# Hand-written order for the last five units of a chunked mLSTM, and a regrouped merge and dispatch behind them

## The chip, the cores and the metric

One core of a Trainium2 chip (trn2) runs the whole program in one launch. The metric is the device time of an execution in microseconds, taken as the median of several runs. TensorE (PE) does the products, VectorE (DVE), ScalarE (ACT) and GpSimd (POOL) the rest; SyncE (SP) issues the DMAs.

## The reference

Three layers in a row, all in float32, on 3072 tokens (4 batches of 768) of width 320.

1. mLSTM: 32 heads (8 per batch) of width 40. Per step `m' = max(f + m, i)`, `C = exp(f + m - m') C + exp(i - m') v k^T`, `n` the same with `k` alone, `y = sigmoid(o) * (C q) / max(|n q|, 1)`.
2. Soft mixture of experts: `logits = x @ phi` (32 slots); a softmax over the tokens (down the columns) mixes tokens into slots (dispatch), eight experts with a hidden width of 1024 and a relu work on four slots each, and a softmax over the slots (along the rows) mixes the results back into tokens (combine).
3. MLP: `relu(x @ w_in)^2 @ w_out` with 2048 hidden columns.

The column softmax needs the maximum over all tokens, so the dispatch can't end before the last token of layer 1 is there.

## The kernel before, in words

Heads are taken in groups of three (the last, group 10, has two), time in six chunks of 128. A pair (g, c) of group and chunk is a unit; there are 66, the last six being (10, 0) to (10, 5). Each goes through the same steps. `e_u` makes the outer products of a chunk on PE, `e_uc` the running state from them (with a mask that keeps each head's own block), `e_mb` and `e_exp` the decay factors (PE, then ACT), `e_sel` their causal cut (POOL), `e_st` the scores (PE), `e_pm` their product with the factors (DVE), `e_inter` the part that comes from earlier chunks' state and `e_av` the part from the chunk itself (PE, both into one PSUM bank for a pair of chunks), `e_num` their sum. `fin(g)` then divides a group's sums by the denominators and multiplies them into the sigmoid in tile `x`.

The loop over the units (from line 947) issues the steps of different units interleaved, scores two units ahead and factors three. All other work of this time is held as generators ("fillers") that yield a letter for the engine they want next: the sigmoids, `fin`, layer 2's tokens of batches 0 to 2, `merge` (which brings the three batches' column maxima together, line 802) and `merge_tr` (transposes of batch 3, line 853). `filler` and `advance` take from them at fixed places of each unit. All waits on semaphores are set by the framework from the order of the program; every engine and SP's queue work in that order.

PSUM is divided into banks by tags: two of `mb`, `st` and `o` each, one `m`, and `ltb` for the logits. A `bank(tag)` that is asked for again waits for all readers of the old contents.

Behind the loop come the last unit's sum (`n1`), `fin_last(2)` for the last two chunks, and what is left of the fillers. Then the tail in straight code: `fold` (line 842) adds the three batches' dispatched rows into partitions 96 to 127; the last 80 columns of batch 3 are transposed (L1110) and copied (L1112); the last logits; the maximum (L1125), the exponentials (L1126), the product L1131 that brings the maxima of four row blocks together, transposes of the exponentials (L1138) and their copy `en` (L1139); the dispatch product L1153, copied by ACT (L1160) and DVE (L1161) from one bank; four products with `comb` (L1166, L1170) and the denominators' (L1171), copied into `sT01` and `sT2` (L1173, L1178); and `ffn_up(0)`, the experts' first product (L1204). `cbuild(tg)` prepares the combine weights of 512 tokens in three parts: a split on DVE (L1071, L1072), four transposes on PE (L1078), a copy on ACT (L1083). `warm(n)` issues n bfloat16 products on the identity (L200) that nobody reads. `ld_w1`, `ld_w2` and `load_wo` issue weight transfers on SP.

The division of the last chunks before, in a few lines:

```python
nc.vector.scalar_tensor_tensor(out=rc, in0=dn, scalar=-1.0, in1=dn, op0=ALU.mult, op1=ALU.max)   # L673
nc.vector.tensor_tensor(out=xv, in0=xv, in1=nv, op=ALU.mult)                                      # L675
nc.vector.tensor_scalar(out=rc, in0=rc, scalar1=1.0, scalar2=2.0, op0=ALU.max, op1=ALU.mult)      # L676
nc.vector.reciprocal(rc, rc)                                                                      # L678
nc.vector.tensor_tensor(out=xv, in0=xv, in1=rc.unsqueeze(3).to_broadcast(...), op=ALU.mult)       # L679
```

Of the kernel before, what the change touches and what calls it, by code (L numbers as in the profile page):

```python
# [44 lines left out]
def kernel(  # L45
# [465 lines left out]
    def e_uc(g, c):  # L511
# [4 lines left out]
        cb = cb01[g, c % 2] if g < 2 else wk.tile([120, nh, DV], F32, tag="cbd", name="cbd", bufs=2)  # L516
        if c == 0:
            nc.vector.tensor_tensor(out=cb[0:nd], in0=uv, in1=hv, op=ALU.mult)
        else:
            if units.index((g, c)) >= NU - 3:  # L520
                nc.vector.tensor_tensor(out=uv, in0=uv, in1=hv, op=ALU.mult)
                nc.vector.scalar_tensor_tensor(
                    out=cb[0:nd],
                    in0=cbds[g, c - 1][0:nd],
                    scalar=dec120[0:nd, g, c : c + 1],
                    in1=uv,
                    op0=ALU.mult,
                    op1=ALU.add,
                )
                cbds[g, c] = cb  # L530
                return
# [50 lines left out]
    def e_num(g, c):  # L582
# [10 lines left out]
        tmp = wk.tile([128, 2, nh, DV], F32, tag="tmp", name="tmp", bufs=1)  # L593
        if n == 1:
            nc.scalar.copy(nums[g][:, 0], pv[:, 0, 0])
        if g == NG - 1 and c == 3:
            for k in range(n):
                for j in range(nh):
                    q0 = 64 + h0 + j
                    nc.scalar.activation(  # L600
                        tmp[:, k, j], pv[:, 1, k, j], AF.Copy, scale=qt3[:, c - 1 + k, q0 : q0 + 1]
# [11 lines left out]
    def fin(g, c0=0, c1=NC):  # L613
# [23 lines left out]
        order = "GG" if g == NG - 1 else "GGDGDD" if len(css) == 3 else "GD" * len(css)  # L637
        k = {"G": 0, "D": 0}
        for e in order:
            yield e  # L640
            i, cs = k[e], css[k[e] if g < NG - 1 else 0]
            k[e] += 1
            if g == NG - 1 and i:
                xv = xb[B1][:, cs, DM - nh * D : DM].rearrange("p c (n d) -> p c n d", d=D)
                eng.tensor_tensor(out=xv, in0=xv, in1=numr[0], op=ALU.mult)
# [19 lines left out]
    def fin_last(k, mid):  # L665
# [4 lines left out]
        rc = wk.tile([128, 2, nh], F32, tag="rcl", name="rcl", bufs=1)  # L670
        nv = num[:, :, :, 0:D]
        xv = xb[B1][:, 2 * k : 2 * k + 2, hh * D : (hh + nh) * D].rearrange("p c (n d) -> p c n d", d=D)
        nc.vector.scalar_tensor_tensor(out=rc, in0=dn, scalar=-1.0, in1=dn, op0=ALU.mult, op1=ALU.max)  # L673
        next(mid)
        nc.vector.tensor_tensor(out=xv, in0=xv, in1=nv, op=ALU.mult)  # L675
        nc.vector.tensor_scalar(out=rc, in0=rc, scalar1=1.0, scalar2=2.0, op0=ALU.max, op1=ALU.mult)  # L676
        finish(mid)
        nc.vector.reciprocal(rc, rc)  # L678
        nc.vector.tensor_tensor(out=xv, in0=xv, in1=rc.unsqueeze(3).to_broadcast([128, 2, nh, D]), op=ALU.mult)  # L679

    def sigm(b):
        for c in range(0, NC, 2):
# [4 lines left out]
            if b == B1:  # L687
                xl = xb[b][:, c : c + 2, DM - groups[NG - 1][1] * D : DM]
# [24 lines left out]
    def logits(kts):  # L713
        for kt in kts:
            kn = KT[kt][1]
            for r in range(NQ):
# [84 lines left out]

    def merge():
# [20 lines left out]
        yield "N"  # L823
        tt3 = mp.tile([96, B1], F32, tag="tt3", name="tt3")
        nc.vector.tensor_tensor(out=tt3, in0=es3, in1=se3, op=ALU.mult)
        cb3 = mp.tile([96, B1, 32], F32, tag="cb3", name="cb3")
        nc.vector.tensor_tensor(
            out=cb3,
            in0=selF[0:96].unsqueeze(1).to_broadcast([96, B1, 32]),
            in1=es3.unsqueeze(2).to_broadcast([96, B1, 32]),  # L830
            op=ALU.mult,
        )
        yield "P"
        t = ltb
        nc.tensor.matmul(t[:, DM : DM + B1], lhsT=sel4f[0:96], rhs=tt3, start=True, stop=True)
        folds.append(cb3)
        yield "N"
        nc.vector.tensor_reduce(out=se4[96:128], in_=t[96:128, DM : DM + B1], axis=AX.X, op=ALU.add)

    folds = []  # L840

    def fold():
        t = bank("st")
        for b in range(B1):
# [3 lines left out]
            if b < B1 - 1:  # L848
                yield
        nc.scalar.copy(xs4[96:128], t[96:128, 0:DM])  # L850
        yield

    def merge_tr():
# [4 lines left out]
        yield "Q"  # L858
        logits([1])
# [83 lines left out]
    for i, (g, c) in enumerate(units):  # L943
# [16 lines left out]
        if i == NU - 2:  # L960
            done.add("last")
            advance("Q", 1)
# [64 lines left out]
        if g == NG - 1 and c in (2, 4):  # L1027
            finish(nm or ())
            nm = None
            f1 = fin(g, c - 2, c)  # L1030
            if c == 2:
                add(f1, ("fin", g), [("sig", B1)])
            else:
                for _ in range(3):
                    next(f1)
# [8 lines left out]
    n1 = e_num(*units[NU - 1])  # L1044
    next(n1)
    finish(n1)
    fin_last(2, f1)
    while fillers:
        advance("W")
        filler("QPNADngG")  # L1050
# [17 lines left out]
    def cbuild(tg, get):  # L1068
        ct = call[:, 4 * tg : 4 * tg + 4, :].unsqueeze(2).to_broadcast([128, 4, 2, 32])
        chl = cp_.tile([128, 4, 2, 2, 32], F32R, tag="chl", name="chl", bufs=2)  # L1070
        nc.vector.tensor_copy(chl[:, :, :, 0, :], ct)  # L1071
        nc.vector.tensor_tensor(  # L1072
# [14 lines left out]
        cbuild(1, lambda: bank("o")),  # L1087
# [5 lines left out]

    def cgo(*tgs):
        for tg in tgs:
            next(cbs[tg], None)
# [3 lines left out]
    for n in (4, 5):  # L1100
        ld_w2(w2p[n], *w2o[2 + n])
    dumt = bank("mb")
    warm(4, dumt)
# [26 lines left out]
    tm = bank("m")  # L1130
    nc.tensor.matmul(tm[:, 0:4], lhsT=sel4f, rhs=mxr, start=True, stop=True)  # L1131
    rm = ca.tile([128, 1], F32, name="rm")
    nc.vector.tensor_reduce(out=rm, in_=tm[:, 0:4], axis=AX.X, op=ALU.max, negate=True)
# [7 lines left out]
    tr_el(0)  # L1141
    es = ca.tile([128, 1], F32, name="es")
    nc.scalar.activation(es, mx4, AF.Exp, bias=rm)
    nc.scalar.copy(el[:, 1, :], lt)
# [4 lines left out]
    next(fd)  # L1149
    xx = bank("st")  # L1150
    for u in range(2):
        for r in range(NQ):
            nc.tensor.matmul(  # L1153
                xx[32 * r : 32 * r + 32, 0:DM],
                lhsT=en[:, 0, u, 32 * r : 32 * r + 32],
# [424 lines left out]
```

## Time and profile before

| | |
|---|---|
| median of 3 runs | 385.25 us (385.08 to 386.76) |
| the profiled execution's own time | 386.99 us |
| its span in the profile | 385.3 us |
| busy share of the span | PE 97%, PEld 87%, DVE 69%, ACT 66%, POOL 27% |
| instructions | 9126 |

A row of a timeline tells when a group of like instructions on one engine began, how long it took with its tail, its line, what it writes and reads, its shape and count; in brackets how long the engine had been idle before it and whose work ended that. Neighbouring groups on PE overlap, since the next begins before the tail of the last is out. The lengths of PE's instructions are modelled.

### The profile page before, as it was taken

To read this page: it belongs to the slowest core of one execution; us is meant where nothing else is said; L and a number is where in the kernel's file an instruction comes from. 1 tells how busy PE (TensorE), PEld (TensorE's weight loads), DVE (VectorE), ACT (ScalarE), POOL (GpSimd) and SP (SyncE) were. 2 spreads that over 40 slices of the span, in tenths; PEclk is the share of its full clock that TensorE was granted. 3 is DMA by queue.
4 is the path that set the end of the run, shared out by engine and by line. 5 is a ranking of instruction groups with operands and counts; after the bars stand their busy time and mean duration, and the time that the engine had idled before them with its cause. 6 is when DMAs were issued, how large, how long until landed. Compare 5 with 4: busy or idle time off the path is not lost.

```text
span 385.3 us, 9126 instructions
## 1 busy us (share of the span) xinstructions
PE 374.1 (97%) x3419; PEld 333.8 (87%) x3419; DVE 265.9 (69%) x597; ACT 256.1 (66%) x585; POOL 102.5 (27%) x208
## 2 busy tenths in 40 slices
PE   8899999999999999999999999999999999999996
PEld 6789999889888886445699899999999999999996
DVE  7878888879888577758688965555555555555551
ACT  7689766668656854455697976676676667667662
POOL 4656866865686466000000000000000000000000
PEclk9899999999999999999999999999999999999999
DMA  6777898899959998599000010020010001002001
GB/s 187 246 267 230 276 308 244 240 331 336 313 173 364 330 350 307 191 382 373 1 2 0 2 68 3 0 70 1 2 53 17 1 2 68 2 1 70 1 2 68
DMA packets 19541, 56.62 MB, mean 147 GB/s; under 512 B 2481, under 2 KB 7561, under 8 KB 19113
## 3 DMA queue, kind: packets, MB, share of 16 engines
q1 hardware_dynamic: 19497, 56.04, 42.8%
q8 instruction: 27, 0.44, 0.5%
q14 instruction: 17, 0.14, 0.1%
HBM read 52.10 MB, written 3.93 MB: 145 GB/s over the span
## 4 chain that ended last, share of the span: by engine, by line
PE 78%; DVE 9%; ACT 4%; POOL 4%; issue 3%; DMA 2%; SPq 0%; DVEq 0%; POOLq 0%; ACTq 0%
PE ps_mb L1478 18%; PE ps_st L1478 17%; PE ps_lt L1478 9%; PE ps_st L474 6%; PE ps_o L1404 4%; PE ps_o L574 3%; PE ps_o L559 3%; PE ps_st L1282 2%; PE ps_m L1404 2%; DVE x L656 2%; DVE p L486 2%; PE ps_st L502 2%; ACT w L457 2%; PE ps_lt L717 1%; POOL w L464 1%
## 5 line engine op out<-in xcount | busy, mean ns | idle before, releaser
L1428 DVE CAST hi<-ring 128x512 fp32r<-128x512 f32 x93 | 39.7, 427 | 60.9 <-ACT ring L1427 52.7
L1429 DVE TENSOR_TENSOR los<-ring,hi 128x512 fp32r<-128x512 f32 x96 | 66.5, 692 | 9.8
L457 ACT ACTIVATE w<-ps_mb,qt 128x128 f32<-128x128 f32 x192 | 56.6, 368 | 15.8 <-PE ps_mb L443 10.4
L1409 ACT ACTIVATE ring<-ps_o 128x512 f32<-128x512 f32 x64 | 38.3, 599 | 34.1 <-PE ps_o L1404 34.1
L1427 ACT ACTIVATE ring<-ring 128x512 f32<-128x512 f32 x93 | 58.8, 632 | 3.0
L474 PE MATMUL ps_st<-par 120*128 120x128 f32 (+1 forms) x384 | 57.6, 286 | 0.0
L1478 PE MATMUL ps_mb<-wohlh,hi 128*128 128x320 f32 x160 | 49.4, 310 | 0.0
L1478 PE MATMUL ps_mb<-wohll,hi 128*128 128x320 f32 x160 | 49.3, 309 | 0.0
L1478 PE MATMUL ps_mb<-wohlh,los 128*128 128x320 f32 x160 | 49.2, 309 | 0.0
L474 PEld LDWEIGHTS ps_st<-par 120*128 120x128 f32 (+1 forms) x384 | 48.6, 194 | 0.0
L1478 PE MATMUL ps_st<-wohll,hi 128*128 128x320 f32 x144 | 44.7, 310 | 0.0
L1478 PE MATMUL ps_st<-wohlh,hi 128*128 128x320 f32 x144 | 44.5, 309 | 0.0
L1478 PE MATMUL ps_st<-wohlh,los 128*128 128x320 f32 x144 | 44.5, 309 | 0.0
L464 POOL TENSOR_SCALAR_AFFINE_SELECT w<-w 128x384 f32<-128x384 f32 (+1 forms) x66 | 36.4, 552 | 19.4 <-ACT w L457 13.6
L486 DVE TENSOR_TENSOR p<-ps_st,w 128x384 f32<-128x384 f32 (+1 forms) x66 | 35.4, 537 | 3.7 <-POOL w L464 2.7
L1409 ACT ACTIVATE ring<-ps_m 128x512 f32<-128x512 f32 x32 | 19.2, 599 | 18.2 <-PE ps_m L1404 18.2
L1478 PEld LDWEIGHTS ps_mb<-wohll,hi 128*128 128x128 f32 x160 | 29.9, 187 | 1.5
L1478 PEld LDWEIGHTS ps_mb<-wohlh,hi 128*128 128x128 f32 x160 | 30.0, 188 | 0.0
L1478 PEld LDWEIGHTS ps_mb<-wohlh,los 128*128 128x128 f32 x160 | 30.0, 188 | 0.0
L574 PE MATMUL ps_o<-par,p 128*64 128x41 f32 x768 | 29.0, 232 | 0.0
L1478 PEld LDWEIGHTS ps_st<-wohll,hi 128*128 128x128 f32 x144 | 27.0, 187 | 2.1 <-issue 0.6
L574 PEld LDWEIGHTS ps_o<-par,p 128*64 128x64 f32 x768 | 25.1, 137 | 3.9
(287 smaller groups left out, 776.1 us busy)
## 6 DMA issues: line engine op xcount, KB each, us to landing
ring<-in_w_dram SPq DMA_DIRECT2D x22, 640.0 KB
stage<-in_w_in_dram SPq DMA_DIRECT2D x10, 512.0 KB
par<-in_w_dram SPq DMA_DIRECT2D x6, 640.0 KB
out_dram<-ring SPq DMA_DIRECT2D x24, 160.0 KB
par<-in_v_s_dram SPq DMA_DIRECT2D x9, 369.0 KB
par<-in_k_s_dram SPq DMA_DIRECT2D x9, 360.0 KB
x<-in_o_gate_dram SPq DMA_DIRECT2D x9, 320.0 KB
par<-in_k_t_dram SPq DMA_DIRECT2D x23, 120.0 KB
```

The source lines that it names most:

```text
L457: nc.scalar.activation(w[:, j, :], mb[:, 128 * j : 128 * j + 128], AF.Exp, bias=qt3[:, c, h0 + j : h0 + j + 1])
L464: nc.gpsimd.affine_select(out=w, in_=w, pattern=[[0, nh], [1, 128]], compare_op=ALU.is_ge, fill=0.0, base=0, channel_multiplier=-1)
L474: nc.tensor.matmul(st[:, 128 * j : 128 * j + 128], lhsT=kbd[g % 2][0:nd, j, ts_], rhs=qin[g][0:nd, ts_], start=True, stop=True,)
L486: nc.vector.tensor_tensor(out=p, in0=sts.pop((g, c))[:, 0 : nh * 128].rearrange("p (n t) -> p n t", n=nh), in1=ws.pop((g, c)), op=ALU.mult,)
L559: nc.tensor.matmul(pos[g, c // 2][:, o0 : o0 + nv], lhsT=qin[g][0:nd, 128 * c : 128 * c + 128], rhs=cbds[g, c - 1][0:nd], start=True, stop ...
L574: nc.tensor.matmul(po[t0 : t0 + 64, o0 : o0 + DV], lhsT=p[:, j, t0 : t0 + 64], rhs=vin[g][:, c, j, :], start=True, stop=True,)
L1404: nc.tensor.matmul(t, lhsT=gst[n][:, 128 * k : 128 * k + 128], rhs=cst[tg], start=True, stop=True)
L1409: nc.scalar.activation(r, t, AF.Relu)
L1427: nc.scalar.activation(r, r, AF.Square)
L1428: nc.vector.tensor_copy(hi, r)
L1429: eng.tensor_tensor(out=lo, in0=r, in1=hi.bitcast(F32), op=ALU.subtract)
L1478: nc.tensor.matmul(acc[u][:, 0:DM], lhsT=l_[:, 128 * u : 128 * u + 128], rhs=wohl[r_, f // 8][:, f % 8, :], start=(f == 0 and a == 0), sto ...
```

## The change

- `e_uc` makes the state with two DVE instructions (mask on the products in PSUM, then the decayed sum) for the last five units, before for the last three. The others use one on DVE and a mask on POOL.
- The loop stops ahead of the last five units, and their steps are written out in an order by hand. `step` takes a filler's next parts.
- `e_num` of group 10 scales the state's part on ACT for chunks 1 and 3 (before for 3 alone).
- `fin(9)` adds its last third on POOL (with the sigmoid's +1 done beforehand on ACT); `fin(10)` is gone: `fin_last` divides all three pairs of chunks, of the first two both multiplies on POOL.
- The merge stops at the exponentials; `rest` makes the fold's weights and the denominators' terms behind `fin_last`, and their product is `tm[:, 16:19]`, in the bank of the maxima's product. The three folds come together.
- The logits' second third comes behind the last transposes; of the last third two row blocks go ahead of the third.
- The transposes of the exponentials stand ahead of the maxima's product; the dispatch product is done in two column halves in two banks, the products with `comb` in two banks.
- The eight `warm` products of the tail are gone, and one block of combine transposes moves behind `ffn_up(0)`, whose terms come in the order 0, 2, 1, 3, 4. Two w2 transfers move ahead of two `load_wo`.

```diff
-            if units.index((g, c)) >= NU - 3:
+            if units.index((g, c)) >= NU - 5:
...
-        if g == NG - 1 and c == 3:
+        if g == NG - 1 and c < NC - 1:
...
     def fin(g, c0=0, c1=NC):
-        order = "GG" if g == NG - 1 else "GGDGDD" if len(css) == 3 else "GD" * len(css)
+        order = "GGDGDX" if g == NG - 2 else "GGDGDD" if len(css) == 3 else "GD" * len(css)
...
-    def fin_last(k, mid):
+    def fin_last(k):
...
+        if k < 2:
+            nc.scalar.activation(rc, dn, AF.Abs)
+        else:
+            nc.vector.scalar_tensor_tensor(out=rc, in0=dn, scalar=-1.0, in1=dn, op0=ALU.mult, op1=ALU.max)
+            nc.vector.tensor_tensor(out=xv, in0=xv, in1=nv, op=ALU.mult)
+        (nc.vector if k == 2 else nc.gpsimd).tensor_scalar(
+            out=rc, in0=rc, scalar1=1.0, scalar2=2.0, op0=ALU.max, op1=ALU.mult
+        )
+        if k < 2:
+            nc.gpsimd.tensor_tensor(out=xv, in0=xv, in1=nv, op=ALU.mult)
+        yield
         nc.vector.reciprocal(rc, rc)
+        (nc.vector if k == 2 else nc.gpsimd).tensor_tensor(out=xv, in0=xv, in1=rb, op=ALU.mult)
...
-    for i, (g, c) in enumerate(units):
+    for i, (g, c) in enumerate(units[: NU - 5]):
...
+    e_u(g, 1)
+    e_mb(g, 4)
+    e_st(g, 3)
+    while w1q:
+        ld_w1(*w1q.pop(0))
+    ld_w2(w2p[2], *w2o[4])
+    e_uc(g, 1)
+    e_pm(g, 3)
+    e_exp(g, 4)
+    step("merge")
+    e_av(g, 0)
+    e_av(g, 1)
+    step("tr", 2)
+    e_inter(g, 1)
+    e_sel(g, 4)
+    step(f9, 3)
+    e_u(g, 2)
+    e_mb(g, 5)
+    e_st(g, 4)
+    e_uc(g, 2)
+    e_pm(g, 4)
+    e_exp(g, 5)
+    e_inter(g, 2)
+    e_sel(g, 5)
+    n1 = e_num(g, 1)
     next(n1)
+    step(f9, 2)
+    e_u(g, 3)
+    e_st(g, 5)
+    e_u(g, 4)
+    ld_w2(w2p[3], *w2o[5])
+    e_uc(g, 3)
+    e_pm(g, 5)
     finish(n1)
+    e_av(g, 2)
+    e_av(g, 3)
+    e_inter(g, 3)
+    e_uc(g, 4)
+    fl = [fin_last(k) for k in range(3)]
+    step(f9, 2)
+    next(fl[0])
+    n3 = e_num(g, 3)
+    next(n3)
+    e_inter(g, 4)
+    e_av(g, 4)
+    e_av(g, 5)
+    e_inter(g, 5)
+    finish(fl[0])
+    finish(n3)
+    next(fl[1])
+    step("tr", 5)
+    n5 = e_num(g, 5)
+    next(n5)
+    finish(fl[1])
+    finish(n5)
+    finish(fl[2])
...
-    for n in (4, 5):
+    for n in range(4, 8):
         ld_w2(w2p[n], *w2o[2 + n])
-    dumt = bank("mb")
-    warm(4, dumt)
+    rest = rests.pop()
+    next(rest)
...
-    next(fd)
-    cgo(0)
-    logits([2])
+    logits([1])
+    logits([2], (0, 1))
+    tt3 = next(rest)
+    logits([2], (2,))
     load_wo(xTw[:, 0 : SLOT // 2], 6, 2)
     next(fd)
-    warm(3, dumt)
+    next(fd)
+    tm = bank("m")
+    nc.tensor.matmul(tm[:, 16 : 16 + B1], lhsT=sel4f[0:96], rhs=tt3, start=True, stop=True)
...
     tr_el(0)
+    nc.vector.tensor_reduce(out=se4[96:128], in_=tm[96:128, 16 : 16 + B1], axis=AX.X, op=ALU.add)
+    nc.tensor.matmul(tm[:, 0:4], lhsT=sel4f, rhs=mxr, start=True, stop=True)
+    nc.vector.tensor_reduce(out=rm, in_=tm[:, 0:4], axis=AX.X, op=ALU.max, negate=True)
     nc.scalar.activation(es, mx4, AF.Exp, bias=rm)
+    finish(fd)
...
+    cgo(0)
+    for m, cs in enumerate((slice(0, 128), slice(128, DM))):
+        xx = bank("st")
...
+        (nc.vector.tensor_copy if m else nc.scalar.copy)(xs4[0:96, cs], xx[0:96, cs])
+    nc.tensor.matmul(tm[:, 8:9], lhsT=sel4f, rhs=tt, start=True, stop=True)
+    tk = [bank("mb"), bank("o")]
...
+        nc.vector.tensor_copy(sk[kt], tk[kt][:, 0:32].rearrange("p (e i) -> p e i", i=4))
...
+    cgo(0, 1)
     load_wo(x3.rearrange("p c d -> p (c d)")[:, 0 : SLOT // 2], 4, 2)
-    for n in (6, 7):
-        ld_w2(w2p[n], *w2o[2 + n])
-    cgo(1, 0)
...
-    def ffn_up(fh, ms_=range(5)):
+    def ffn_up(fh, ms_=(0, 2, 1, 3, 4)):
...
-    cgo(1, 2)
+    cgo(0, 2)
...
+    cgo(1, 1)
```

## Rows read from the trace of the kernel before

**Rows 1.** Busy time by stage: stage, length, engines, granted clock, DMA share, GB/s.

```profile
142.90:150.00 7.10, 6.84 (x94) 5.81 (x93) 6.21 (x25) 3.60 (x14) 4.36 (x12) 1.00 0.80 273
155.00:160.10 5.10, 4.60 (x42) 2.90 (x41) 2.46 (x13) 2.38 (x7) 0.00 (x0) 1.00 0.33 89
160.10:182.20 22.10, 22.10 (x240) 9.67 (x239) 16.70 (x43) 11.93 (x21) 1.90 (x2) 1.00 0.94 374
190.00:380.00 190.00, 189.31 (x1231) 184.54 (x1230) 115.85 (x203) 129.62 (x223) 0.00 (x0) 1.00 0.05 18
```

**Rows 2.** Chain that ended last, 145 to 161 us: start, length, what.

```profile
145.31 0.51 PE ps_st L474 x4
...
145.93 0.30 DVE cu L533
```

**Rows 3.** Timeline of PE: start, length, line, tiles, shapes, count [idle before <-releaser].

```profile
148.84 0.67 PE L574 MATMUL ps_o<-par,p 128*64 128x41 f32 x16
149.76 0.45 PE L559 MATMUL ps_o<-cbd,par 80*128 80x82 f32 x2 [0.26 <-DVE cbd L522]
...
151.32 0.89 PE L717 MATMUL ps_lt<-xTw,phs 120*32 120x256 f32 x6 [0.46 <-ACT xTw L711]
152.15 0.61 PE L200 MATMUL ps_mb<-ident 128*128 128x256 bf16 x4
...
155.60 0.36 PE L1131 MATMUL ps_m<-mxr,sel 128*128 128x4 f32 x2 [0.50 <-DVE mxr L1129]
155.81 0.36 PE L1138 MATMUL ps_mb<-ident,el 96*128 96x96 f32 x2
156.10 0.72 PE L845 MATMUL ps_st<-xs,cb 96*32 96x320 f32 x2
156.63 1.28 PE L1153 MATMUL ps_st<-x,en 128*32 128x320 f32 x12
...
159.51 0.63 PE L1078 MATMUL ps_o<-ident,chl 128*128 128x128 f32 x4
160.08 4.50 PE L1204 MATMUL ps_st<-ring,x 128*32 128x512 f32 x40
```

**Rows 4.** Timeline of DVE, 147 to 159 us.

```profile
147.53 0.25 DVE L521 TENSOR_TENSOR ps_mb<-ps_mb,hm 80x82 f32<-80x82 f32 x1
147.88 0.30 DVE L522 SCALAR_TENSOR_TENSOR cbd<-cbd,dec,ps_mb 80x82 f32<-80x82 f32 x1
148.10 0.41 DVE L486 TENSOR_TENSOR p<-ps_st,w 128x256 f32<-128x256 f32 x1
148.43 0.71 DVE L656 SCALAR_TENSOR_TENSOR x<-x,numr 128x240 f32<-128x240 f32 x2
...
150.61 0.33 DVE L611 TENSOR_TENSOR num<-ps_o,tmp 128x164 f32<-128x164 f32 x1
...
151.14 0.29 DVE L675 TENSOR_TENSOR x<-x,num 128x160 f32<-128x160 f32 x1
...
152.03 0.51 DVE L679 TENSOR_TENSOR x<-x,rcl 128x160 f32<-128x160 f32 x1
...
154.58 0.42 DVE L1125 TENSOR_REDUCE nmx<-ps_lt 96x1 f32<-96x256 f32 x1
...
156.21 0.36 DVE L1139 COPY en<-ps_mb 128x192 f32<-128x192 f32 x1
...
158.28 0.35 DVE L1161 COPY xs<-ps_st 96x192 f32<-96x192 f32 x1 [1.46 <-ACT xs L1160]
```

**Rows 5.** Timelines of ACT and POOL, the same stretch.

```profile
147.86 0.85 ACT L600 ACTIVATE tmp<-ps_o,qt 128x41 f32<-128x41 f32 x4 [0.57 <-PE ps_o L559]
...
151.84 0.52 POOL L645 TENSOR_TENSOR x<-x,numr 128x160 f32<-128x160 f32 x1
```

**Rows 6.** Timeline of PE near the start, and a one-us stage behind its idle time.

```profile
12.40 0.47 PE L502 MATMUL ps_st<-wv,par 128*120 128x123 f32 x2 [1.26 <-DVE p L486]
...
13.00:14.00 1.00, 1.00 (x6) 1.00 (x6) 0.97 (x3) 0.83 (x3) 0.35 (x1) 0.50 0.94 263
```

More of the change, by code (lines that the diff above doesn't have):

```diff
@@ L711, in moe_kt, with logits @@
             nc.scalar.copy(xT[0:kn, 128 * c0 : 128 * c0 + w], t[0:kn, 0:w])
-    def logits(kts):
+    def logits(kts, rs=range(NQ)):
         for kt in kts:
             kn = KT[kt][1]
-            for r in range(NQ):
+            for r in rs:
                 nc.tensor.matmul(
@@ L800 @@
     sel4f = sel4.rearrange("p r s -> p (r s)")
+    folds, rests = [], []
     def merge():
@@ L822, in merge, with rest @@
         nc.scalar.activation(es3, mx3, AF.Exp, bias=pm[0:96])
-        yield "N"
         tt3 = mp.tile([96, B1], F32, tag="tt3", name="tt3")
-        nc.vector.tensor_tensor(out=tt3, in0=es3, in1=se3, op=ALU.mult)
         cb3 = mp.tile([96, B1, 32], F32, tag="cb3", name="cb3")
[L827 to L840, printed above, removed]
+        def rest():
+            nc.vector.tensor_tensor(
+                out=cb3,
+                in0=selF[0:96].unsqueeze(1).to_broadcast([96, B1, 32]),
+                in1=es3.unsqueeze(2).to_broadcast([96, B1, 32]),
+                op=ALU.mult,
+            )
+            folds.append(cb3)
+            yield
+            nc.vector.tensor_tensor(out=tt3, in0=es3, in1=se3, op=ALU.mult)
+            yield tt3
+        rests.append(rest())
     def fold():
@@ L1026 @@
                 add(fin(g1), ("fin", g1), [("sig", b) for b in batches(g1)])
[L1027 to L1035, printed above, removed]
         if i >= QI:
@@ L1043, with step @@
     rt128 = ca.tile([128, 1], F32, name="rt128")
-    n1 = e_num(*units[NU - 1])
-    next(n1)
-    finish(n1)
[L1047 to L1050, printed above, removed]
+    def step(key, n=1):
+        for _ in range(n):
+            f = next(f for f in fillers if f[2] == key)
+            t = next(f[0], None)
+            if t is None:
+                fillers.remove(f)
+                done.add(key)
+            else:
+                f[1], f[3] = split(t)
+    g = NG - 1
+    f9 = ("fin", g - 1)
+    e_u(g, 1)
[23 more added lines that the diff above has]
+    n1 = e_num(g, 1)
+    next(n1)
+    step(f9, 2)
[5 more added lines that the diff above has]
+    e_pm(g, 5)
+    finish(n1)
+    e_av(g, 2)
[20 more added lines that the diff above has]
+    finish(fl[2])
     fd = fold()
@@ L1092 @@
     ]
+    begun = set()
     def cgo(*tgs):
         for tg in tgs:
+            if tg not in begun:
+                begun.add(tg)
+                next(cbs[tg])
             next(cbs[tg], None)
@@ L1148 @@
     nc.vector.tensor_tensor(out=tt, in0=es, in1=se4, op=ALU.mult)
[L1149 to L1155, printed above, removed]
-                rhs=x3[:, 2 * r + u, :],
-                start=(u == 0),
-                stop=(u == 1),
-            )
-    nc.scalar.copy(xs4[0:96, 0:128], xx[0:96, 0:128])
-    nc.vector.tensor_copy(xs4[0:96, 128:DM], xx[0:96, 128:DM])
@@ L1162 @@
-    cgo(0, 1)
-    warm(1, dumt)
-    t = bank("st")
+    cgo(0)
+    for m, cs in enumerate((slice(0, 128), slice(128, DM))):
+        xx = bank("st")
+        for u in range(2):
+            for r in range(NQ):
+                nc.tensor.matmul(
+                    xx[32 * r : 32 * r + 32, cs],
+                    lhsT=en[:, 0, u, 32 * r : 32 * r + 32],
+                    rhs=x3[:, 2 * r + u, cs],
+                    start=(u == 0),
+                    stop=(u == 1),
+                )
+        (nc.vector.tensor_copy if m else nc.scalar.copy)(xs4[0:96, cs], xx[0:96, cs])
@@ L1165 @@
+    nc.tensor.matmul(tm[:, 8:9], lhsT=sel4f, rhs=tt, start=True, stop=True)
+    tk = [bank("mb"), bank("o")]
+    t = tk[0]
+    sk = [sT01[:, k].rearrange("p (e w) -> p e w", w=32)[:, :, 0:4] for k in range(2)]
     for kt in range(2):
         nc.tensor.matmul(
-            t[:, 32 * kt : 32 * kt + 32], lhsT=xs4[:, 128 * kt : 128 * kt + 128], rhs=comb, start=True, stop=True
+            tk[kt][:, 0:32], lhsT=xs4[:, 128 * kt : 128 * kt + 128], rhs=comb, start=True, stop=True
         )
+        nc.vector.tensor_copy(sk[kt], tk[kt][:, 0:32].rearrange("p (e i) -> p e i", i=4))
```

57 lines of the change are left out of this document (20 added, 37 removed).

## The prediction, made before the change was run

> **What bounds the kernel now.** I read the busy time by stage first, to see whose stage the change touches. From 160.1 us on TensorE is busy 22.10 of 22.10 us, and 189.31 of 190 in the long last stage [rows 1]: whatever the stretch before gains reaches the end one for one, and no weight transfer ends a wait there. The changed stretch runs from unit (10,1)'s first product at 142.9 to the first up-projection product at 160.08 [rows 3]. Here too TensorE is mostly busy (6.84 of 7.10 us, then 4.60 of 5.10) [rows 1], so the second view is its own timeline: the reader is to look for the brackets. There are three idle gaps on it, 0.26, 0.46 and 0.50 us, and eight filler products L200 at 0.11 each (four take 152.15 to 152.60) [rows 3]. **That is a ceiling: 1.22 + 0.9 = 2.1 us**, 0.55% of the run, if all idle and all filler went and no new wait came. Third I read what the gaps wait for: DVE's states, ACT's copy, and the column maximum with its small products [rows 3, 4].
>
> One behaviour is needed throughout. L533 wants only the product L502, but starts behind L474, which writes other columns of the same PSUM bank [rows 2]; and DVE's copy L1161 starts after ACT's copy from the same bank (idle 1.46, released by ACT) although their columns differ [rows 4]. So in this kernel two engines take turns in a bank whatever the columns are. I use this for the new order.
>
> **The change part by part**, with trace times of before.
>
> *Recurrence.* (10,1) and (10,2) now make their state by L521 and L522 on DVE, not L533 plus a mask on POOL. The pair takes 0.57 of DVE (147.53 to 148.10) [rows 4], against 0.30 for L533 [rows 2]. Up to the score products of (10,4) TensorE's order issues the same work, so DVE again starts (10,2)'s state at 145.93 [rows 2]. From there DVE has: pair 0.57, L486 0.33, half of the L656 pair 0.35, pair 0.57, L486 0.33, L611 of chunk 1 about 0.3, then L521 0.35 and L522 0.30 [rows 4]. The last state is there at 148.9; before, it released TensorE at 149.76 [rows 3]. Moved away from this piece are chunk-1 and chunk-3 products with the q factor (L604 to ACT's L600, four in 0.85 [rows 5]) and the merge's sums.
>
> *A new wait.* Units (10,4) and (10,5) take the `o` bank of (10,0) and (10,1), whose last reader is L611 of chunk 1. That used to be done early; now it stands behind two states and a L486 and ends at about 148.35. e_inter(10,4), sixteen L574 and e_inter(10,5) queue behind it on TensorE: 148.39 + 0.29 + 0.60 + 0.45 = 149.73, where it was 149.76 + 0.45 = 150.21 [rows 3] (0.45 and 0.67 are such groups with their tails; the next one starts 0.29 and 0.60 behind their start). Of 0.8 us won on DVE, 0.5 is left.
>
> *Last normalisation.* DVE's L604 (0.33) then stands at 150.1, but the reciprocal of chunks 2 and 3 is issued before the last L611, and it waits for a relay: ACT's four products (start 148.45, 0.85), L611 0.33, an absolute value on ACT and a maximum on POOL (0.2 each, an estimate from the smallest DVE rows). That relay ends at 150.25. So the last L611 ends near 150.7, before at 150.94 [rows 4]: 0.25 won. From there to the end of L679 it was 1.60 us. Two multiplies of 160 numbers, both by DVE: L675 0.29, L679 0.51 [rows 4]. The long one ran beside POOL's L645 [rows 5]. After the change POOL works there as well (it has both multiplies of chunks 0 to 3, then a memset), so at worst nothing is saved; without a slowdown the tail is 1.2. I take 1.4, the middle: L679 ends at 152.1 instead of 152.54, ends 151.9 and 152.3.
> The Trainium skill (GPSIMD Engine Reference, section 1, Specifications) says that POOL shares its SBUF interfaces with DVE instructions that have two SBUF inputs; the pair 0.29 and 0.51 agrees, and by that rule alone the end would be 152.3 and the sum 0.2 worse.
>
> *Transposes and logits.* The first four transposes no longer queue for the last chunk; only two stand behind L679. After them: DVE's copy 0.42, the last third of the logits (two passes, some 0.6), hops. I take 1.65 us from L679 to L1125 (ends 1.55 and 1.8; before 154.58 - 152.54 = 2.04). L1125 starts at 153.75: **0.83 us won**. logits([1]) fits between on TensorE, since ACT's copies for it come when they came before, by 151.32 [rows 3] and shortly after.
>
> *From the maximum to the first up-projection product.* Before: 160.08 - 154.58 = 5.50 us. After, counted from L1125: en's copy may start at 1.42 instead of 1.63, as L1131 (0.21, from 155.60 to 155.81 [rows 3]) no longer stands ahead of L1138. But L1131 now writes the bank from which DVE reads the merged sum, and that read is queued on DVE behind en's copy (0.36): 1.42 + 0.36 + some 0.2 = 1.97, where L1131 started at 1.02. Behind it on TensorE stand the last fold (0.52) and the dispatch products: these begin at 2.70 instead of 2.05. This is the price of the new wait, **0.65**. Dispatch in two halves has twice as many instructions: 1.27 before, from 1.27 (same columns) to 1.7; I take 1.5, with the first fold's bank freed by ACT in it. The halves lie in two banks, so DVE's copy no longer waits for ACT's: 0.74 becomes 0.39. Copy to first product was 1.44, with one block of transposes of the combine weights (0.57, 159.51 to 160.08 [rows 3]) in it; one PSUM read less in a row and the denominators' product moved ahead leave 1.2. Sum 2.70 + 1.50 + 0.39 + 1.20 = 5.79, **0.29 lost**; ends 5.4 and 6.1.
>
> *Moved behind.* Of the two blocks of transposes ahead of the up-projection, that of group 1 now stands behind it, where TensorE has no idle time [rows 1]: **0.57 lost**. Its place before lay under the wait for the dispatch copies, so nothing is won there. Its DVE and ACT parts, three instructions, fall in a stage where DVE is busy 16.70 and ACT 11.93 of 22.10: free.
>
> *Edits at nothing.* The two weight transfers into the new buffer move ahead of two others on SP and into a stretch where the DMA engines are busy 33% [rows 1]; the xTw transfer slips behind the last logits, but wo_narrow(6) first reads it in the down-projection. The last w1 half passes one w2 half in SP's queue, and both are needed only after 160. The wider +1 on ACT (120 more numbers in each of two chunks, once) comes with the sigmoid of batch 3, before the stretch. Last third of group 9 on POOL: it ends at about 148.5, and its readers come at 150.1; if that cover were gone it would cost the same 0.5 on the path. Without the fillers only the clock could change (below).
>
> **Sum:** -0.83 + 0.29 + 0.57 = +0.03 us. The profiled execution took 386.99 us, its span 385.30; the median of the runs is 385.25, 1.74 below that execution, and I apply the difference to the median: **385.3 us**. The ends of the terms add to -0.9 and +0.8: 384.4 to 386.1.
>
> **Rivals.** *No new wait decides* (0.20). If the bank of the merged sum doesn't hold up L1131, the 0.65 goes, and if the `o` bank comes free earlier and the tail isn't slowed by POOL, 0.5 more: 1.2 us won, 384.1, and at most the ceiling, 383.1. For it speaks that DVE has idle time for every one of these reads; against it L1161 and L533. It decides if dispatch begins 2.1 us after L1125 or less.
>
> *The clock falls* (0.12): the case that ends slower. Near the start TensorE stood idle 1.26 us, and behind it the granted clock read 0.50, the 1.2 GHz level (five rows like that from 12 to 17: 0.95, 0.50 three times, 0.84, so 3.4 us in all) [rows 6]. The change takes out the fillers and opens gaps of about 0.6 us at 147.7 and 150.8 and another between folds and L1131. If the clock falls at 151 to 154, every product on this path takes twice as long: at most half of 3.4, **1.7 us, 387.0**, some more if it falls twice. Against it: the gap of 0.50 at 155.1, in a stretch that is busy 4.60 of 5.10 with the fillers, left the clock at 1.00 [rows 1, 3].
> The Trainium skill (TensorE: Matmul & The Clock Gate, Part 1) states that the slow clock is the default and activity releases it, which speaks against taking fillers out; the row at 13 us agrees, no row shows it for gaps of 0.6 us.
>
> *POOL and DVE get in each other's way* (0.08): four multiplies more on POOL, each able to stretch a DVE instruction by 0.2 (0.29 to 0.51 [rows 4]): +0.7, 386.0.
>
> **How the numbers follow.** Forecast, with its terms' ends: 0.60. The bound for faster or slower is 0.5%, 1.9 us, about what a measurement of this kernel can tell from no change. To be faster by that nearly the whole ceiling must be won: two fifths of the first rival, 0.08. Slower by that: the clock falls for longer than at the start or meets the third case, 0.07. The rest, 0.85, is the same. The range, 383.6 to 386.9, holds the forecast's own, the third rival, most of the first and the weaker half of the second.
>
> **What would show it.** Right: e_inter(10,4) on TensorE waits for DVE's L611; L1125 starts near 153.75; L1131 is released by the merged sum's reduction and dispatch begins 2.7 us after L1125; the up-projection starts near 159.5 and its second half about when it did before, 5 us after 160.08. Wrong: the second half starts over a microsecond earlier, or a granted clock under 1.00 between 145 and 160, or TensorE idle for a DMA after 170.

## The result, and the profile after

| | before | after |
|---|---|---|
| median of the runs | 385.41 us (384.86 to 386.88, 22 runs) | 387.94 us (385.10 to 391.47, 22 runs) |
| ratio after to before | | 1.0052, 95% interval 1.0032 to 1.0072 |
| the profiled execution's own time | 386.99 us | 385.23 us |
| its span | 385.3 us | 383.5 us |

The change makes the kernel slower by about 0.5%; 387.94 lies 1.0 us above the end of the range that was given (386.9) and 2.6 above the forecast. The ratio leaves out the two slowest runs of after (391.44 and 391.47); they belong to the pattern below all the same.

What strikes first is that the profile shows none of this. The profiled execution of after is one of its fastest, and shorter than that of before. The runs one by one, with the mean granted clock of TensorE over the execution, show it:

```
mean clock     runs of after   time, us
0.999 - 1.000   4              385.10 - 385.54
0.994 - 0.996   5              386.00 - 387.39
0.989 - 0.991   8              387.87 - 388.59
0.987           3              389.73 - 390.30
0.982           2              391.44 - 391.47
```

This is a staircase. A low stretch in these traces (1.2 GHz, clock 0.50) lasts 3.41 us, as from 12.90 to 16.31 us in before [rows 6]; one of them lowers the mean by 0.5 x 3.41 / 385 = 0.0044. So 0.982 is four such stretches, 0.987 three, 0.991 two, 0.995 one. Four of 22 executions had none, and a step costs about 1.5 us ((391.45 - 385.37) / 4). **At full clock (a mean of 0.998 or more) the median of after is 385.37 us, where 385.3 was forecast.** What is missing to 1.000 is in after's profile a fall at 382.09 us, when TensorE has no more work. The runs of before that belong to this pair have no clock on record; 20 of the 22 lie under 386 us, median 385.35. In the first batch below before had full clock in 30 of 33 runs, median 385.16, and the other three lay at 386.77 to 386.86.

The page of after, its first line and the clock by 40 slices of the span:

```profile
span 383.5 us, 9138 instructions
...
PEclk9999999999999999999999999999999999999999
```

Both executions have to be set at one point before they are compared. Two rows of before's timeline of TensorE, not shown so far: the product of unit (10,2), and the up-projection's second half:

```profile
144.89 0.30 PE L502 MATMUL ps_st<-wv,par 128*80 128x82 f32 x2
...
165.13 1.06 PE L1204 MATMUL ps_o<-ring,x 128*32 128x512 f32 x8
```

Timeline of TensorE, after, with the product of (10,2) in its first row (start, length with the tail, line, names, shapes, count, and in brackets idle time before and what ended it):

```profile
142.68 0.31 PE L502 MATMUL ps_st<-wv,par 128*80 128x82 f32 x2
...
146.04 0.42 PE L559 MATMUL ps_o<-cbd,par 80*128 80x82 f32 x2 [0.51 <-DVE num L611]
146.39 0.67 PE L574 MATMUL ps_o<-par,p 128*64 128x41 f32 x16
146.98 0.45 PE L559 MATMUL ps_o<-cbd,par 80*128 80x82 f32 x2
...
153.56 0.39 PE L1202 MATMUL ps_m<-mxr,sel 128*128 128x4 f32 x2 [0.63 <-DVE se L1201]
153.87 0.46 PE L853 MATMUL ps_st<-xs,cb 96*32 96x320 f32 x1
153.88 0.53 PE L1218 MATMUL ps_st<-x,en 128*32 128x128 f32 x9
...
155.10 0.85 PE L1218 MATMUL ps_st<-x,en 128*32 128x192 f32 x12 [0.51 <-ACT xs L857]
...
157.11 0.66 PE L1133 MATMUL ps_o<-ident,chl 128*128 128x128 f32 x4
157.69 4.50 PE L1264 MATMUL ps_st<-ring,x 128*32 128x512 f32 x40
...
163.33 2.78 PE L1264 MATMUL ps_o<-ring,x 128*32 128x512 f32 x24
```

L1202 is L1131 of before, L1218 is L1153, L1133 is L1078 and L1264 is L1204. In after the product of (10,2) comes 144.89 - 142.68 = 2.21 us earlier: the slow start of before's execution [rows 6], not the change: in e3 below, which has before's order and no low stretch near the start, that product starts at 142.92. The span is 1.8 shorter, so from that product on after loses 0.4. To be seen in the rows: two new waits of the two kinds that were expected (`o` bank, 0.51; the merged sum, 0.63), and one that was not priced, 0.51 for ACT's copy of the fold, in the middle of the dispatch. Two short ones, 0.21 and 0.28, stand ahead of the transposes L1170, which read the last multiplies.

DVE, and then ACT, in the same stretch of after (L1188 is the maximum, L1125 before; L1201 the merged sum's reduction; L857 the copy of a fold's rows, L850 before):

```profile
148.13 0.30 DVE L611 TENSOR_TENSOR num<-ps_o,tmp 128x164 f32<-128x164 f32 x1
...
149.44 0.33 DVE L686 TENSOR_TENSOR x<-x,rcl 128x160 f32<-128x160 f32 x1
...
151.47 0.42 DVE L1188 TENSOR_REDUCE nmx<-ps_lt 96x1 f32<-96x256 f32 x1 [0.64 <-PE ps_lt L725]
...
152.96 0.36 DVE L1198 COPY en<-ps_mb 128x192 f32<-128x192 f32 x1 [0.62 <-PE ps_mb L1197]
153.34 0.17 DVE L1201 TENSOR_REDUCE se<-ps_m 32x1 f32<-32x3 f32 x1
153.98 0.16 DVE L1204 TENSOR_REDUCE rm<-ps_m 128x1 f32<-128x4 f32 x1 [0.48 <-PE ps_m L1202]
...
156.04 0.35 DVE L1225 COPY xs<-ps_st 96x192 f32<-96x192 f32 x1 [0.57 <-PE ps_st L1218]
```

```profile
154.18 0.29 ACT L1206 ACTIVATE es<-mx,rm 128x1 f32<-128x1 f32 x1 [1.69 <-DVE rm L1204]
154.63 0.42 ACT L857 COPY xs<-ps_st 32x320 f32<-32x320 f32 x1 [0.16 <-PE ps_st L853]
```

Stages of after (columns as in [rows 1]): TensorE is full behind 157.69, as it was, and no transfer has become late.

```profile
151.47:157.69 6.22, 4.93 (x49) 3.03 (x47) 3.58 (x16) 1.81 (x6) 0.00 (x0) 1.00 0.88 319
157.69:170.00 12.31, 12.31 (x114) 4.58 (x113) 7.74 (x23) 6.33 (x11) 1.84 (x2) 1.00 0.81 299
170.00:175.00 5.00, 5.00 (x76) 2.60 (x76) 3.65 (x8) 3.64 (x7) 0.00 (x0) 1.00 0.97 378
```

### The profile page after: what moved, and what is told of

Read it like the earlier page. It is cut to its first block, busy times and chain, and to the rows that moved or that the text cites. A ratio compares the mean times of both kernels' runs of the same rounds, so it can differ in the third digit from the quotient of the medians.

```text
span 383.5 us, 9138 instructions
## 1 busy us (share of the span) xinstructions
PE 372.2 (97%) x3423; PEld 332.5 (87%) x3423; DVE 263.5 (69%) x598; ACT 256.4 (67%) x587; POOL 102.7 (27%) x207
## 4 chain that ended last, share of the span: by engine, by line
PE 83%; DVE 5%; POOL 4%; ACT 3%; issue 2%; DMA 1%; SPq 0%; POOLq 0%; DVEq 0%
PE ps_mb L1539 18%; PE ps_st L1539 17%; PE ps_lt L1539 9%; PE ps_st L474 8%; PE ps_o L574 4%; PE ps_o L1465 4%; PE ps_o L559 3%; PE ps_st L1343 2%; PE ps_st L502 2%; PE ps_m L1465 2%; PE ps_lt L200 2%; PE ps_mb L443 2%; PE ps_lt L725 1%; POOL w L464 1%; DVE x L656 1%
## 5 line engine op out<-in xcount | busy, mean ns | idle before, releaser
L464 POOL TENSOR_SCALAR_AFFINE_SELECT w<-w 128x384 f32<-128x384 f32 (+1 forms) x66 | 37.2, 564 | 18.6 <-ACT w L457 13.4
```

The costliest lines, as they stand in the source:

```text
L464: nc.gpsimd.affine_select(out=w, in_=w, pattern=[[0, nh], [1, 128]], compare_op=ALU.is_ge, fill=0.0, base=0, channel_multiplier=-1)
```

## The experiments

Two questions: what brings the clock down, and what the order is worth without it. Three answers to the first were set against each other: the eight fillers taken out; the wait of the maxima's product for the merged sum (with the dispatch wait that follows from it); the wait for the `o` bank. The table gives for each kernel the number of its runs at full clock, since that, more than the median, tells the theories apart. Runs of before beside them: 385.30 us (first four kernels), 385.59 (next four), 385.34 (last two); 75 of these 86 at full clock. No kernel leaves out work; the fillers' products are read by nobody.

```
kernel                                       median   ratio (95%)              at full clock
e1  after, unchanged                         388.12   1.0067 (1.0041, 1.0092)   2 of 10
e2  after + the eight fillers                385.90   1.0022 (1.0003, 1.0040)   9 of 12
e3  before - the eight fillers               385.11   0.9997 (0.9989, 1.0006)  11 of 11
e4  after, maxima before merged sum          385.03   1.0001 (0.9986, 1.0016)   8 of 12
e5  e4 + early sum of chunk 1                384.86   0.9989 (0.9975, 1.0002)   9 of 12
e6  after + early sum of chunk 1             388.56   1.0074 (1.0047, 1.0102)   1 of 7
e7  after + fillers in the tail's two waits  385.68   1.0002 (0.9990, 1.0014)  10 of 12
e8  before - fillers + merged-sum wait       387.72   1.0048 (1.0025, 1.0071)   2 of 12
e9  e5 + third fold early                    384.66   0.9982 (0.9968, 0.9995)   9 of 12
e10 e9 + first transposes early              384.47   0.9973 (0.9961, 0.9985)  12 of 12
```

**e1: after, unchanged**, for an execution with a low stretch in its profile.

> The changed kernel once more, for the spread of its times against the granted clock. Theory F (the clock falls because the eight filler products are gone): times spread over several us again, each run's time going with its mean granted clock at about 1.5 us per 0.0044 of clock (one stretch of 3.4 us at half clock), the runs with a clock of 0.999 or 1.000 at the time of the kernel before, within 0.4 us. Theory W (the order itself is longer, the clock only follows): the runs at full clock are slower than the kernel before by 1 us or more.

Its profiled execution took 386.74 us, mean clock 0.994. Timeline of TensorE, then the stages around the fall:

```profile
146.76 0.42 PE L559 MATMUL ps_o<-cbd,par 80*128 80x82 f32 x2 [0.51 <-DVE num L611]
...
148.93 1.11 PE L716 MATMUL ps_m<-ident,x 128*120 128x128 f32 x4
```

```profile
144.90:148.30 3.40, 2.90 (x46) 2.36 (x47) 2.97 (x13) 1.24 (x7) 2.90 (x7) 1.00 0.77 241
148.30:151.70 3.40, 3.40 (x18) 2.09 (x12) 2.60 (x9) 1.20 (x3) 2.09 (x5) 0.50 0.93 355
```

The clock reads 0.50 from 148.30 to 151.72, behind a stretch with the `o` wait in it. The four transposes L716 take 1.11 us where after's first profile has 0.65. The low stretch that was in no profile is thus in the changed stretch here.

**e2: after with the eight fillers back** where before had them, and **e3: before without them**.

```diff
+    dumt = bank("mb")
+    warm(4, dumt)
     rest = rests.pop()
...
     nc.tensor.matmul(tm[:, 16 : 16 + B1], lhsT=sel4f[0:96], rhs=tt3, start=True, stop=True)
+    warm(3, dumt)
...
+    warm(1, dumt)
     nc.tensor.matmul(tm[:, 8:9], lhsT=sel4f, rhs=tt, start=True, stop=True)
```

> The changed kernel with the eight filler products put back: four ahead of the last transposes, three behind the product of the merged sums, one ahead of the denominators' product. Theory F: the spread shrinks to that of the kernel before (under 2 us from lowest to highest), median within 0.7 us of the kernel before. Theory W or theory G (the gaps of the new order are too long for so few fillers): the spread stays at 4 us or more and the median 2 us or more above the kernel before.

```diff
-    dumt = bank("mb")
-    warm(4, dumt)
...
-    warm(3, dumt)
...
-    warm(1, dumt)
```

> The kernel before without its eight filler products, nothing else. Theory F: it gets the spread of the changed kernel, median 1 to 3 us above the kernel before, mean granted clocks between 0.98 and 1.00. Theory G: the old order has its gaps elsewhere, so it stays within 0.5 us of the kernel before and its clock at 0.995 or more.

e3 settles that the missing fillers alone are not the cause: eleven of eleven runs at full clock, 385.11 us. Its timeline has one long gap ahead of the maxima's product:

```profile
153.30 0.35 PE L1128 MATMUL ps_m<-mxr,sel 128*128 128x4 f32 x2 [0.94 <-DVE mxr L1126]
```

In e2 the tail's two waits are what they are in after, and yet nine of twelve runs are at full clock:

```profile
155.11 0.49 PE L200 MATMUL ps_mb<-ident 128*128 128x256 bf16 x3
...
156.40 0.39 PE L1205 MATMUL ps_m<-mxr,sel 128*128 128x4 f32 x2 [0.63 <-DVE se L1204]
...
157.95 0.85 PE L1221 MATMUL ps_st<-x,en 128*32 128x192 f32 x12 [0.51 <-ACT xs L857]
```

So neither half does much alone: the missing fillers without the new waits leave 11 of 11 runs at full clock (e3), the new waits with the fillers 9 of 12 (e2), both together 6 of 32 (after and e1). The falls of e2's profiled execution are at 12.41 and at 148.94, ahead of every filler of the tail. Neither expectation for e2 came out whole: its runs spread over 3.2 us, and its median lies 0.6 above before's. Its runs at full clock spread to 386.37, for which no cause was found.

**e4: after, with the product of the maxima issued ahead of the merged sum's reduction**, so that the wait of 0.63 goes; this is the only edit.

```diff
-    nc.vector.tensor_reduce(out=se4[96:128], in_=tm[96:128, 16 : 16 + B1], axis=AX.X, op=ALU.add)
     nc.tensor.matmul(tm[:, 0:4], lhsT=sel4f, rhs=mxr, start=True, stop=True)
     rm = ca.tile([128, 1], F32, name="rm")
     nc.vector.tensor_reduce(out=rm, in_=tm[:, 0:4], axis=AX.X, op=ALU.max, negate=True)
+    nc.vector.tensor_reduce(out=se4[96:128], in_=tm[96:128, 16 : 16 + B1], axis=AX.X, op=ALU.add)
```

> The changed kernel with the product of the maxima issued ahead of the reduction of the merged sums, so that the product no longer waits for DVE's read of its bank. From the prediction's step: the dispatch products begin about 2.1 us behind the start of the maximum's reduction instead of 2.4 to 2.7, and runs at full clock are 0.3 to 0.65 us faster than the changed kernel's. Theory F: the spread over several us stays.

385.03 us: two instructions in another order give back 3.1 us of e1's 388.12. Only 0.45 of that is path (the medians at full clock are 385.35 in e1, of two runs, and 384.90 here); the rest is clock. Timeline of TensorE in e4:

```profile
147.90 0.42 PE L559 MATMUL ps_o<-cbd,par 80*128 80x82 f32 x2 [0.51 <-DVE num L611]
...
155.32 0.31 PE L1201 MATMUL ps_m<-mxr,sel 128*128 128x4 f32 x2
155.56 0.73 PE L853 MATMUL ps_st<-xs,cb 96*32 96x320 f32 x2
155.93 0.64 PE L1218 MATMUL ps_st<-x,en 128*32 128x128 f32 x12
156.79 0.85 PE L1218 MATMUL ps_st<-x,en 128*32 128x192 f32 x12 [0.22 <-ACT xs L857]
```

The wait is gone, and with it more than half of the one in the dispatch (0.22 for 0.51): ACT's copy stands behind an exponential that needs the maxima. The two falls that are left in this execution are at 12.93 and, behind the `o` wait, at 149.47.

**e5: e4 with the sum of chunk 1 issued before the state of (10,3)**, which takes the `o` wait down; **e6: that alone**, with the tail's waits left in.

```diff
     ld_w2(w2p[3], *w2o[5])
+    finish(n1)
     e_uc(g, 3)
     e_pm(g, 5)
-    finish(n1)
     e_av(g, 2)
```

> The run with the early product of the maxima, and in addition the sum of chunk 1 issued on DVE ahead of the state of (10,3), so that the bank for (10,4) is free when TensorE gets there. Theory L (the clock falls where TensorE stands idle in the two new waits, 0.5 us before e_inter(10,4) and 0.6 us before the product of the maxima): no clock fall in the stretch any more, all runs within 1.1 us of each other but for the rare fall near the start, median 0.2 to 0.8 us below the kernel before. Theory T (the tail alone sets the falls): as the early product alone, about 3 of 12 runs with two falls.

> The changed kernel with only the early sum of chunk 1; the wait ahead of the product of the maxima stays. Theory L: falls become rarer but don't vanish, median between 385.5 and 387.5. Theory T: the spread of the changed kernel stays, median 387.5 to 388.5, most clocks at 0.991.

The pair separates the tail from what lies ahead of it. With the `o` wait cut to 0.17 and the tail as it was, one run of seven is at full clock; with the tail's wait gone too, nine of twelve, and the other three are at 0.995 to 0.996, as the odd runs of before are. Of the two expectations for e6 the one by which the tail alone sets the falls (387.5 to 388.5) comes nearer to its 388.56 than the one that gives the `o` wait a part (385.5 to 387.5). Timeline and stages of e6:

```profile
146.30 0.42 PE L559 MATMUL ps_o<-cbd,par 80*128 80x82 f32 x2 [0.17 <-DVE cbd L522]
...
149.81 0.41 PE L1170 MATMUL ps_o<-ident,x 128*80 128x128 f32 x2 [0.54 <-POOL x L686]
...
154.15 0.39 PE L1202 MATMUL ps_m<-mxr,sel 128*128 128x4 f32 x2 [0.63 <-DVE se L1201]
...
155.70 1.50 PE L1218 MATMUL ps_st<-x,en 128*32 128x192 f32 x12 [0.51 <-ACT xs L857]
...
159.96 5.59 PE L1264 MATMUL ps_st<-ring,x 128*32 128x512 f32 x40
```

```profile
152.00:155.40 3.40, 2.42 (x24) 1.26 (x21) 1.79 (x9) 1.03 (x4) 0.00 (x0) 1.00 0.93 364
155.40:162.20 6.80, 6.50 (x38) 3.54 (x42) 4.32 (x22) 2.73 (x6) 0.00 (x0) 0.50 0.53 188
```

The clock falls at 155.39, inside the second wait of the tail (155.19 to 155.70), and stays down twice as long as elsewhere, through the dispatch, the combine products and into the up-projection, which takes 5.59 us for after's 4.50. No fall is left at 148. But the early sum does not take idle time away there, it moves it: ahead of L1170 TensorE now waits 0.54 us for POOL's multiply L686, where after waits 0.21, in e5 as in e6.

**e7: after with fillers in the tail's two waits**, and nothing shortened.

```diff
     tr_el(0)
+    warm(5, dumt)
...
     for m, cs in enumerate((slice(0, 128), slice(128, DM))):
+        warm(4 * m, dumt)
         xx = bank("st")
```

> The changed kernel with its waits left and nine filler products put exactly into the two waits of the tail: five behind the transposes of the exponentials, four between the two dispatch halves. Theory L: fillers in the right place do what removing the waits does, so the tail's falls go (median 385.0 to 386.0, as with the early product), and at full clock it is no slower than the changed kernel by over 0.3 us. If only the waits' length matters and not that TensorE is idle in them, the median stays near 388.

```profile
152.85 0.71 PE L200 MATMUL ps_mb<-ident 128*128 128x256 bf16 x5
153.65 0.39 PE L1204 MATMUL ps_m<-mxr,sel 128*128 128x4 f32 x2
...
154.62 0.61 PE L200 MATMUL ps_mb<-ident 128*128 128x256 bf16 x4
155.20 0.85 PE L1221 MATMUL ps_st<-x,en 128*32 128x192 f32 x12
```

The waits last as long as before (the dispatch's second half starts 1.23 us behind its first in this timeline, 1.22 in after's), yet ten of twelve runs are at full clock and the ratio to before falls from 1.0067 to 1.0002. The waits' length on the path was never what the 2.5 us were.

**e8: before, without its fillers and with the merged sum's wait alone**: that sum's product goes into the maxima's bank, its reduction behind the copy `en`, the maxima's product behind that, and so behind the transposes L1128. Everything else is before.

```diff
...
-        nc.tensor.matmul(t[:, DM : DM + B1], lhsT=sel4f[0:96], rhs=tt3, start=True, stop=True)
         folds.append(cb3)
...
-        nc.vector.tensor_reduce(out=se4[96:128], in_=t[96:128, DM : DM + B1], axis=AX.X, op=ALU.add)
+        folds.append(tt3)
...
+    tm = bank("m")
+    nc.tensor.matmul(tm[:, 16 : 16 + B1], lhsT=sel4f[0:96], rhs=folds[1], start=True, stop=True)
...
     tr_el(0)
+    nc.vector.tensor_reduce(out=se4[96:128], in_=tm[96:128, 16 : 16 + B1], axis=AX.X, op=ALU.add)
+    nc.tensor.matmul(tm[:, 0:4], lhsT=sel4f, rhs=mxr, start=True, stop=True)
```

> The kernel before without its eight filler products (no slower than with them, by the earlier run) and with one part of the change alone: the merged sums' product in the bank of the maxima, their reduction behind en's copy, the product of the maxima behind that. Theory L: this one wait is enough to bring falls into the old order: some runs with a clock of 0.996 or 0.991 beyond the 1 in 11 that fall near the start, median 0.5 to 3 us above the kernel before. The prediction's sum, clock apart: about 0.65 us slower at full clock, less what the maxima's product no longer standing ahead of the transposes gives back (0.2).

```profile
154.90 0.39 PE L1128 MATMUL ps_mb<-ident,el 96*128 96x96 f32 x2 [0.68 <-ACT el L1121]
155.91 0.39 PE L1133 MATMUL ps_m<-mxr,sel 128*128 128x4 f32 x2 [0.63 <-DVE se L1132]
...
156.63 1.84 PE L1147 MATMUL ps_st<-x,en 128*32 128x320 f32 x9
```

```profile
156.40:159.80 3.40, 3.40 (x21) 1.82 (x14) 1.34 (x6) 1.40 (x5) 0.00 (x0) 0.50 0.22 24
```

387.72 us, two of twelve at full clock, and these two at 384.89 and 385.51, inside before's own spread. One wait, put into the old kernel without its fillers, makes a regression as large as the change's (1.0048, beside 1.0052 and 1.0067), and makes it through the clock. The 0.45 us of path that were expected besides (0.65 less 0.2) do not show in these two runs, which are too few to tell. Beside e3, from which it differs by this edit, one gap of 0.94 has become two, of 0.68 and 0.63.

**e9: e5 with the third fold issued with the other two**, its ACT copy ahead of the exponential; **e10: e9 with the first transposes of the combine weights between the dispatch and the `comb` products**.

```diff
     next(fd)
     next(fd)
+    next(fd)
     tm = bank("m")
...
+    finish(fd)
...
     nc.scalar.activation(es, mx4, AF.Exp, bias=rm)
-    finish(fd)
```

> The run with both waits taken away, and the third fold issued with the first two, so that ACT copies the folds before it needs the maxima and the second dispatch half finds its bank free (that wait was 0.51 us on TensorE in the changed kernel, 0.22 with the early product). Theory L: no falls but the rare one near the start, median 0.2 to 0.4 us below that run, 0.5 to 1.1 below the kernel before. If the waits on TensorE there were not on the path that sets the end, the median equals that run's within 0.1 us.

```diff
+    cgo(0)
     nc.tensor.matmul(tm[:, 8:9], lhsT=sel4f, rhs=tt, start=True, stop=True)
...
-    cgo(0, 1)
+    cgo(1)
```

> As the run with the early folds, and the transposes of combine group 0 issued between the dispatch products and the products with comb, where TensorE waits for DVE's copy. By the prediction's step (such a block costs 0.57 where TensorE has no idle time and nothing under that wait): 0.2 to 0.5 us faster than the run with the early folds. If DVE's copy comes as soon as the block has been issued, no difference.

```profile
153.79 1.29 PE L1219 MATMUL ps_st<-x,en 128*32 128x128 f32 x24 [0.30 <-DVE en L1200]
155.28 0.63 PE L1133 MATMUL ps_o<-ident,chl 128*128 128x128 f32 x4 [0.20 <-DVE chl L1127]
...
156.87 4.50 PE L1266 MATMUL ps_st<-ring,x 128*32 128x512 f32 x40
```

In e9 and in e10 the dispatch runs through in 1.29 us. 384.47 us is the best of all, 0.27% under before, and the interval ends under 1 (0.9961 to 0.9985). The step from e9 to e10, 0.19 us, is smaller than the spread of either and is not claimed.

## Why the prediction was wrong, and where it was right

**The recurrence and the last normalisation held.** Counted from L502, e_inter(10,5) ends at 146.98 + 0.45 - 142.68 = 4.75 us; before, 150.21 - 144.89 = 5.32 [rows 3]: 0.57 won, forecast 0.5. The `o` bank's new wait is there, released by L611 as said. The last L611 ends 0.30 earlier (forecast 0.25), and from it to the end of the last multiply are 149.77 - 148.43 = 1.34 us, forecast 1.4 between 1.2 and 1.6. The maximum starts 151.47 - 142.68 = 8.79 behind L502, before 154.58 - 144.89 = 9.69 [rows 4]: **0.90 won, forecast 0.83**.

**The new wait of L1131 was right in kind, and nearly in place.** L1202 starts 2.09 us behind the maximum (forecast 1.97), released by the merged sum's reduction. The dispatch starts at 2.41, not 2.70: the third fold and the first dispatch products run side by side (both from 153.87) where the forecast put one behind the other.

**The dispatch was mis-sized.** "I take 1.5, with the first fold's bank freed by ACT in it": it lasts 155.95 - 153.88 = 2.07 us, above the upper end of 1.7, since its second half stands 0.51 for ACT's fold copy L857. The bank was named, and ACT's queue not followed: that copy comes behind the exponential L1206, which needs L1204, which needs L1202, so the merged sum's wait is paid a second time. From the maximum to the up-projection are 6.22 us (2.41 + 2.07 + copy 0.44 + rest 1.30) for a forecast of 5.79, just past its end of 6.1: 0.72 lost, not 0.29.

**The block moved behind cost what was said.** First to second half of the up-projection is 163.33 - 157.69 = 5.64 us; before, 165.13 - 160.08 = 5.05: 0.59 lost, forecast 0.57.

**The sum** is -0.90 + 0.72 + 0.59 = +0.41 in the profiled execution, forecast +0.03. At full clock the medians differ by 0.2 (385.37 and 385.16), and hardly at all from the pair's own runs of before (385.35). So the rival in which no new wait decides is out by its own point: the dispatch begins at 2.41, not at 2.1 or less. POOL and DVE in each other's way is out as well; the tail was shorter than forecast. There DVE's multiply L678 and POOL's L686 both started at 148.54: DVE's took 0.32 us and POOL's 0.63, where the same POOL line took 0.45 at 147.34. In before it was DVE's L679, started behind POOL's L645, that took the longer time, 0.51; the forecast knew only that case. The ends that the forecast gives with its terms add to -0.69 and +0.66, not to -0.9 and +0.8; the median lies outside either.

**The step that failed** is the one on which the forecast rested without a term: "Without the fillers only the clock could change", with the clock as a rival at 0.12, priced at one low stretch, 1.7 us, "some more if it falls twice". 18 of 22 executions had low stretches, most of them two or more. The price of one was about right (1.5); the number and the chance were not. Two readings led there:

- The evidence against it was one gap of 0.50 us at 155.1 with the clock at 1.00 [rows 1, 3]. That is one gap in one execution. e3 shows that even one gap of 0.94 leaves the clock at full speed in 11 of 11 runs; e8 shows that two of 0.68 and 0.63, with 0.4 us of work between them (154.90 to 155.28), do so in only 2 of 12. The forecast listed three new gaps and weighed them by that one.
- The new wait was priced as path, 0.65 us. Its path was worth 0.36 (2.41 against 2.05). As idle time of TensorE in a place where there is idle time already, it was worth 2.5 us in the median, together with the dispatch wait that follows from it: e8 has the merged sum's wait alone, e4 takes it away, e7 fills both.

The named cause itself was right as a pair: the forecast's rival blamed the fillers taken out together with the new gaps, and neither does much alone (e3 and e2). Of the gaps, e4, e7 and e8 put the falls on the tail's two waits. The `o` wait precedes the falls at 148.30, 148.94 and 149.47 in the profiles of e1, e2 and e4; after's and e7's profiles have it and no fall, and that it costs runs by itself is not shown.

The Trainium skill (TensorE: Matmul & The Clock Gate, Part 1) has the slow clock as what an idle engine is given and activity as what takes it away. The trace agrees in direction, with short gaps: ahead of the fall at 155.39 in e6 TensorE had been busy 2.42 of 3.40 us, with no gap over 0.63. The forecast cited this rule against the change, and gave it little weight because no row showed it for gaps of 0.6 us.

The waits themselves come from two engines taking turns in a bank. The Trainium skill (PSUM — Partial Sum Buffer, section "PSUM bank collisions raise a hardware error") asks for exactly this, by bank and quarter of the partitions rather than by address. The waits that the framework set agree that columns do not matter: L1202 writes columns 0 to 3 and waits for the read of 16 to 18.

**Open.** Which of the executions falls, and where, differs from run to run, and only profiled executions show the place. Why one gap of 0.94 leaves the clock and two shorter ones take it was not settled; nor do two gaps always take it: 0.54 and 0.28 ahead of L1170 in e5, e6, e9 and e10 are followed by no fall there. Which of the tail's two waits weighs more was not run. What the `o` wait costs by itself is not told from the noise (8 of 12 runs at full clock with it in e4, 9 without it in e5).

## What to carry to other kernels

A wait that a new order opens on TensorE has two prices: its length on the path, and the clock, if it joins other idle time nearby; the second was many times the first here (2.5 us beside 0.36). Products that nobody reads can look worthless as long as the gaps are few (e3), and be what holds the clock once a new gap is there (e2). One profiled execution can't show it, so read the granted clock of every run and compare medians at equal clock. When results are regrouped into a shared PSUM bank, follow the bank's last reader through that reader's own queue; issuing the reader behind the waiting product (e4), or work in the gaps (e7), made nearly all of the difference.

## What the runs showed of the hardware that was not expected

- The spread of a kernel's times is a staircase in granted clock: 385.4, 386.5, 388.1, 390.1 and 391.5 us are the middles of after's runs with none to four low stretches.
- Before has the step too, in 11 of 86 runs, at 386.6 to 387.2 us. Its profiled execution (386.99) was of this kind, with the fall at 12.90; falls at 12.41, 12.93 and 13.05 are in the profiles of e2, e4 and e8.
- A low stretch can run on: in e6 it lasted 6.83 us, twice 3.41, although TensorE was busy 6.50 of 6.80 us in it.
- What fillers are worth depends on the gaps around them: with the new waits there, eight at before's places gave 9 of 12 runs at full clock (e2) and nine in the two waits 10 of 12 (e7), where 6 of 32 had it without any; in before, taking them out changed nothing (e3). Which places are better these runs do not tell.
- A fold (96 rows in) and a dispatch product (128 rows in), both of 32 columns out, run side by side on TensorE: L853 at 153.87 and L1218 at 153.88, 0.46 and 0.53 us long (the lengths are modelled), where the program has them in a row.
